# RWKV7 attention into a mixture of experts: raw V and R of the fourth unit loaded ahead of its raw W, those of the fifth behind it, and both turned ahead of the decay for tokens

## The chip, the cores and the metric

The kernel runs on one core of a Trainium2 chip. The metric is the device time of one execution in microseconds (us); less is better. The core has a matrix engine (TensorE, PE in the profile), three engines for elementwise work (VectorE or DVE, ScalarE or ACT, GpSimd or POOL), and SyncE (SP), which here issues nearly all DMA transfers. Each engine works through its own list of instructions in order; engines wait for one another by semaphores.

## The reference

Two stages follow one another. The first is a recurrence over time for each batch and head, with a 40 x 40 state:

```python
# r, k, v, w, a, b: (B=4, H=8, S=768, D=40) float32
for t in range(S):
    y[:, :, t] = einsum('bhd,bhde->bhe', rt, state)
    Sa = einsum('bhde,bhe->bhd', state, at)
    state = state * wt[:, :, None, :] - einsum('bhd,bhe->bhde', Sa, bt)
    state = state + einsum('bhd,bhe->bhde', vt, kt)
```

The second takes y as x with N = 3072 tokens and D = 320 features through a mixture of E = 4 experts with F = 1024 hidden features:

```python
p = domain_probs / (domain_probs.sum(-1, keepdims=True) + 1e-09)
for e in range(E):
    h = maximum(x @ w1[e], 0.0)
    out += p[:, e:e + 1] * (h @ w2[e])
```

## The kernel before

**Units.** Time is cut into 12 chunks of 64 steps and the batch into 2 pairs, so there are 24 units; unit u is chunk u // 2 of pair u % 2, with 16 sequences (2 batches of 8 heads). Inside a unit the recurrence is replaced by matrices: products of W up to each step (G), scores between the steps of the unit, and a triangular system that is solved by doubling in Z and M. Between units of one pair only the state is passed on. When a unit's Y is there, its tokens go through the experts, in pieces that are put between the attention's steps to keep TensorE fed.

**Stages of a unit.** The generator `within` (from line 407) prepares a unit in stages, each ended by a `yield`:

- Stage 1 turns raw W (as loaded, features not yet on the partitions) into G with VectorE's 32 x 32 stream transpose (`turn_raw`, L245) and scans it to running products (L443).
- Stage 2 is the decay for tokens: TensorE turns G back to tokens (`pg`), VectorE multiplies by natural W (`gp`, L454) and takes the reciprocal (L455).
- Stage 3 makes `n_tok` (L476) and `k_tok` (L481) from gp and natural B and K, turns raw A into `AT` (L245) and multiplies it by G (L485), copies natural V into `VC`, and, from unit 3 on, turns raw V and R into `VT` and `RT` by `turn_rv`.
- Stage 4 has TensorE turn n_tok and k_tok (`pNT`, `pKT`), ScalarE copy them out (`NT`, `KT`), TensorE multiply RT with VT (`pc`, the scores of R against V) and NT and KT with AT (`pfe`), and VectorE copy the causal halves (`VC`, `ET`).

`PADDED` is 3: units 0 to 2 bring V and R in by another way (padded tiles turned by TensorE), and unit 3, the fourth, is the first to load them raw. `EARLY` is 5.

After that `substitute` solves the triangular system (M on VectorE, Z on GpSimd, L585 and L598), `merge` turns the result (`Qc`, `QTc`, then `pY`, `Yq`, `pQ`), and `step` carries the state on (`prn`, `RH`, `psat`, `SX`, `pxr`, `pdy`, Y, state). In `mixture_of_unit` and `mixture_of_chunk` TensorE makes `ph`, ScalarE applies the ReLU (`hs`), TensorE makes `po` or `p`, and VectorE evicts it with the gate into `osb` (L795, L797). From later units on VectorE also adds pairs of hs into `a` (L903), and the experts' weights are summed accordingly (`sums`, `w`, L869).

**Buffers.** Raw W, A, R and V have one buffer each: a unit's raw tile can be loaded when the unit before has turned its own. VT, NT and KT share three buffers, RT has two, AT two. PSUM for the experts has three buffers (two for ph, one for p or po).

**Order.** TensorE's instructions run in the order of the program. On VectorE, ScalarE and SP a scheduler sets the order from its own estimate of times, save where `pin` keeps an instruction behind the one before it: in `within` up to unit 3 (L411) and, for G, again from unit 8. From unit 4 on the stages' instructions on VectorE are therefore the scheduler's to place.

**Loads.** `load_raw` returns the issues of a unit's raw tiles in the order of the letters it is given: 4 issues for W or A, 8 for V or R, since the sequences of V and R are put in another order for the two halves. The runs of one issue are 72 or 48 floats long. `go` issues them on SP at once; what is in `later` is issued by `begin_later`, in the next turn of the loop. In the code, unit 3's raw W is issued while unit 2 is prepared, raw A, V and R after its natural tiles; in the loop over u, unit u + 3 has raw W and A issued at once and raw V and R put into `later`.

Of the kernel before, what the change touches and what calls it, by code (L numbers as in the profile page):

```python
# [15 lines left out]
def kernel(  # L16
# [145 lines left out]
    PADDED = 3  # L162
# [27 lines left out]
    units = []  # L190

    def begin(u):
        q = Unit()
        q.u, q.c, q.bp = u, u // (B // 2), u % (B // 2)
        q.b = [2 * q.bp, 2 * q.bp + 1]
        q.start, q.end = q.c == 0, q.c == NC - 1
        q.apart = u >= EARLY + 2
        q.n = {}
        units.append(q)
        return q  # L200
# [38 lines left out]
    def go(moves, eng=None):  # L239
        for move in moves:  # L240
            move(eng or nc.sync)
# [106 lines left out]
    def by(x, n):  # L348
        return x.rearrange("p (h e) -> p h e", e=n)
# [3 lines left out]
    def turn(name, src, pinned=False):  # L353

        p = big(name)
        for j in range(NJ):
            ins = transpose(out=p[:, j * P:(j + 1) * P], in_=src(j), identity=ident[:])
            if pinned and j == 0:
                tc.keep_in_program_order(ins)
        return p  # L360

    def tok(x):
        return lambda j: x[:, 2 * j:2 * j + 2, :].rearrange("p h e -> p (h e)")
# [42 lines left out]
    def within(q):  # L406
# [10 lines left out]
        ahead = G[:, 1:2 * NJ * L + 1].rearrange("p (j i t) -> p i j t", i=2, t=L)  # L417
# [21 lines left out]
        if q.u == 1:  # L439
            yield  # L440
            VT = turn_rv()
# [7 lines left out]
            pin(turn_raw(q.AT[:], n["rawA"][:]))  # L449
        yield  # L450

        pg = by(turn("pg", tok(Gv), q.u == 2)[:], 64)[:, :, 0:D]
        gp = sb.tile([P, H, D], FP32, name="gp")
        pin(nc.vector.tensor_tensor(out=gp[:], in0=pg, in1=n["W"][:], op=ALU.mult))  # L454
# [32 lines left out]
        q.VC = VCs()  # L487
        if q.u > 0:
            nc.scalar.copy(out=q.VC[:, :, 0:D], in_=token_V())
        if q.u >= PADDED:  # L490
            VT = turn_rv()
        yield

# [2 lines left out]
        if q.u == 2:  # L496
            VT = turn_rv()
# [49 lines left out]
    def substitute(q, eng, between=None, during=None):  # L547

        blocks = sb.tile([P, H, Q], FP32, name="blocks")
        for i in range(P // Q):  # L550
            move = nc.scalar.copy if i >= 2 else nc.vector.tensor_copy
            tc.keep_in_program_order(move(out=blocks[quarter(i)], in_=q.F[quarter(i), :, quarter(i % 2)]))  # L552
        q.below = belows()
        for i in (1, 3):
            tc.keep_in_program_order(nc.gpsimd.tensor_copy(out=q.below[quarter(i)], in_=q.F[quarter(i), :, 0:Q]))  # L555
        M = sb.tile([P, Q, Q], FP32, name="M")
        cols = blocks[:].rearrange("p h c -> p c h")[:, :, None, :].to_broadcast([P, Q, 4, H])
        ins = nc.vector.transpose(out=M[:], in_=cols)  # L558
        tc.keep_in_program_order(ins)


        pairs = M[:].rearrange("p (c two) r -> p c two r", two=2)
        on_diag = M[:].rearrange("p c r -> p (c r)")[:, Q + 1::2 * (Q + 1)]
        tc.keep_in_program_order(nc.vector.memset(on_diag, 0.0))

        Z = sb.tile([P, 4, Q // 4, Q], FP32, name="Z")
        q.Z = Z[:, 0]
        by_second = Z[:, 1:3].rearrange("p x k r -> p (x k) r")
        below = M[:].rearrange("p c r -> p (c r)")[:, 1::2 * (Q + 1)]
        ins = nc.vector.tensor_tensor(  # L570
            out=by_second, in0=pairs[:, :, 1, :], in1=below[:, :, None].to_broadcast([P, Q // 2, Q]), op=ALU.mult,
        )
        tc.keep_in_program_order(ins)
        ins = nc.vector.tensor_tensor(out=pairs[:, :, 0, :], in0=pairs[:, :, 0, :], in1=by_second, op=ALU.add)  # L574
        tc.keep_in_program_order(ins)
        run(between)
        at_once = eng is nc.vector
        for x in (0, 3) if at_once else (0,):
            tc.keep_in_program_order(eng.tensor_copy(out=Z[:, x], in_=unit_cols[:]))
        for j in range(0, Q, 2):  # L580
            if during:
                during(j)
            n, m = j // 4 + 1, Q - 1 - j
            here = 3 * (j // 2 % 2) if at_once else 0
            ins = eng.tensor_tensor(  # L585
                out=Z[:, 1:3, 0:n, j + 1:Q], in0=M[:, j:j + 2, None, j + 1:Q].to_broadcast([P, 2, n, m]),
                in1=Z[:, here, 0:n, j:j + 2].rearrange("p k x -> p x k")[:, :, :, None].to_broadcast([P, 2, n, m]),
                op=ALU.mult,
            )
            if j == 0:  # L590
                tc.keep_in_program_order(ins)
            z = Z[:, :, 0:n, j + 1:Q]
            if at_once:
                terms = z[:, 0:3] if here == 0 else z[:, 1:4]
                eng.tensor_reduce(out=z[:, 3 - here], in_=terms.rearrange("p x k r -> p k r x"), op=ALU.add, axis=AX.X)  # L595
            else:
                for x in range(1, 3):
                    eng.tensor_tensor(out=z[:, 0], in0=z[:, 0], in1=z[:, x], op=ALU.add)  # L598
        if at_once:

            odd, even = (Z[:, x].rearrange("p k (r four) -> p k r four", four=4)[:, :, :, 1:3] for x in (3, 0))
            eng.tensor_copy(out=even, in_=odd)
# [431 lines left out]
    def scores_of(u):  # L1034
        run(ws[u], 1)
        yield
# [34 lines left out]
    def during_second(j):  # L1071
# [4 lines left out]
        if j == 12:  # L1076
            run(norm)

    substitute(units[1], nc.vector, scores_of(1), during_second)
    m, s = merge(units[1]), begin_step(1)  # L1080
    run(m, 1)
    run(ws[2], 1)
    go(load_raw(begin(3), "W"))
    mix(2)
    run(ws[2], 1)
    run(m, 1)
# [4 lines left out]
    run(s, 2)  # L1091
    run(ws[2], 1)
    load(units[3], "WBKV")
    go(load_raw(units[3], "AVR"))
    run(ws[2], 2)
    substitute(units[2], nc.gpsimd)
    mix(1)
# [8 lines left out]
    for u in range(1, NU):  # L1106
        in_order[0] = True
        q = units[u]
        m = s_next = w = w_next = iter(())
        if u + 1 < NU:  # L1110
            m, s_next = merge(units[u + 1]), begin_step(u + 1)
            w_next = ws[u + 1]
        if u + 2 < NU:
            w = ws[u + 2]

        def gap(n, pieces=None):
            at = 4 * u + n
            run(sum_ops, sums_at.get(at, 0))
            mix((1 if at in sparse else 2) if pieces is None else pieces)

        early = u < EARLY
        if early:
            begin_later(len(later))
        ahead = u + 3 < NU and u in range(EARLY, EARLY + 3)
        if ahead:
            go(load_raw(begin(u + 3), "W"))
        if early:
            lead()
        run(w_next, 99 if early else 1)
        run(s, 1)  # L1130
        gap(0)


        if early:
            run(s, 1)
        run(w, 1)
        if not early:
            run(w_next)
            run(s)

        if early:
            run(w, 1)
            gap(1, 2 if u + 1 == EARLY else None)
            run(s)
        if u == 1:
            mixture_of_unit(q)
        elif q.bp:
            mixture_of_chunk(units[u - 1:u + 1], chunks_x[q.c])
        if not early:
            begin_later(len(later))  # L1150
            run(w, 1)
            lead()
            todo[:2] = todo[1::-1]
            gap(1)
            run(m, 1)

        if u + 3 < NU:
            go(load_raw(units[u + 3] if ahead else begin(u + 3), "A" if ahead else "WA"))
            load(units[u + 3], "WBKV")
            later.extend(load_raw(units[u + 3], "VR"))  # L1160
        run(w, 2)

        soon = u in (2, 3, 4)
        if soon:
            run(w, 1)
        if early:
            run(m, 1)
        else:
            run(m, 1)
            run(s_next, 1)  # L1170
            lead()
            run(m, 1)
            if u + 3 < NU:
                ws.append(within(units[u + 3]))
                run(ws[u + 3], 1)
        if soon:
            substitute(units[u + 2], nc.gpsimd)
        gap(2)

        if u == 1:  # L1180
            run(s_next, 1)
            run(m, 1)
        if not soon:
            run(w, 1)
        if not soon and u + 2 < NU:
            with sooner(not early):
                substitute(units[u + 2], nc.gpsimd)
        if not early:
            lead()
            run(s_next, 1)  # L1190
        if early:
            run(w, 1)
        if early:
            ws.append(within(units[u + 3]))
            run(ws[u + 3], 1)
            if u > 1:
                run(m, 1)
                run(s_next, 1)
            run(m)
            gap(3, 1)  # L1200
            run(s_next, 1)
        else:
            begin_later(len(later))
            gap(3)
        s = s_next
# [31 lines left out]
```

## Time and profile before

| | |
|---|---|
| median of 3 runs | 1095.37 us (1095.02 to 1099.68) |
| the profiled execution | 1096.91 us |
| its span in the profile | 1095.2 us |
| mean granted TensorE clock | 0.988 |
| TensorE's idle time where it waits for turned R (100 to 330 us) | 2.2 us in 2 waits |
| SP's issues of unit 3's raw V and R | 91.71 to 101.35 us |
| SP's issues of unit 4's raw V and R | 123.34 to 132.90 us |

The profile is one execution; its times are microseconds from the start of its span, and 1.7 us lie around the span. A line of the timeline gives start, duration, engine, line of the kernel, operation, output <- inputs, and in brackets the idle time of the engine before it with what ended it. "issue" there is a wait for nothing that the profile shows.

### The profile page before, as it was taken

Reading aid. Unit: us, or ns where it says so; the run is one execution under the profiler, and the core shown is the slowest. Engines: PE = TensorE matmul, PEld = TensorE weight load, DVE = VectorE, ACT = ScalarE, POOL = GpSimd, SP = SyncE. Lnnn points to the kernel's source line nnn. Section 1 sums busy time; section 2 is a strip of 40 time slices with the busy share of each in tenths; the row PEclk is TensorE's granted clock in tenths of the full one; section 3 lists DMA queues with packets and bytes.
Section 4 is the critical chain, followed back from the end, with each engine's and each line's share of the span. In section 5 each row is a group of like instructions: output and inputs, shape, how many; then the busy total and the mean of one; then the engine's idle time right before and its main releaser. Section 6 shows DMA issues by size and latency. Waiting matters only on the chain.

```text
span 1095.2 us, 38536 instructions
## 1 busy us (share of the span) xinstructions
PE 1068.1 (98%) x16102; PEld 959.0 (88%) x16102; DVE 759.0 (69%) x1551; ACT 353.4 (32%) x956; POOL 490.3 (45%) x1274
## 2 busy tenths in 40 slices
PE   7798999999999999999999999999999999999998
PEld 6677788889998999999999999989999999998887
DVE  7676569887776777767768768767777676544343
ACT  2432444234223333333233242343333332221110
POOL 5206577763472562653643634735625536420000
PEclk8799999999999999999999999999999999999999
DMA  7876545434444463454454454444543532322320
GB/s 118 236 231 142 131 91 131 107 77 108 120 119 105 110 144 97 103 146 97 100 133 105 106 122 106 115 99 105 131 103 85 149 89 60 99 71 79 107 75 13
DMA packets 268869, 122.19 MB, mean 112 GB/s; under 512 B 213736, under 2 KB 242072, under 8 KB 268696
## 3 DMA queue, kind: packets, MB, share of 16 engines
q1 hardware_dynamic: 265416, 119.12, 43.4%
q8 instruction: 127, 2.08, 0.8%
q10 hardware_dynamic: 3280, 0.61, 0.4%
q14 instruction: 46, 0.38, 0.1%
HBM read 111.79 MB, written 3.93 MB: 106 GB/s over the span
## 4 chain that ended last, share of the span: by engine, by line
PE 92%; DVE 4%; ACT 1%; DMA 1%; issue 1%; SPq 0%; DVEq 0%; ACTq 0%
PE ph L76 39%; PE p L76 31%; PE pdy L76 3%; PE psat L76 2%; PE pxr L76 2%; PE po L76 2%; PE prn L76 2%; PE pfe L76 1%; PE pc L76 1%; PE pQ L76 1%; PE pev L76 1%; PE pg L79 1%; PE pY L76 1%; DVE Z L595 1%; PE pe L76 1%
## 5 line engine op out<-in xcount | busy, mean ns | idle before, releaser
L76 PE MATMUL ph<-xT,w1p 128*128 128x256 f32 (+3 forms) x3040 | 443.9, 375 | 3.7 <-issue 3.6
L76 PEld LDWEIGHTS ph<-xT,w1p 64*64 64x64 f32 (+1 forms) x3040 | 337.7, 162 | 59.3 <-issue 18.9
L598 POOL TENSOR_TENSOR Z<-Z 128x31 f32<-128x31 f32 (+7 forms) x704 | 254.8, 362 | 55.2
L903 DVE TENSOR_TENSOR a<-hs 128x512 f32<-128x512 f32 x220 | 153.3, 714 | 105.9 <-ACT hs L784 105.9
L784 ACT ACTIVATE hs<-ph 128x512 f32<-128x512 f32 (+1 forms) x208 | 117.1, 564 | 332.0 <-PE ph L76 331.7
L585 POOL TENSOR_TENSOR Z<-M,Z 128x62 f32<-128x62 f32 (+7 forms) x352 | 148.6, 422 | 99.0 <-DVE M L574 73.1
L76 PE MATMUL p<-sums,a 128*128 128x160 f32 x1056 | 164.9, 299 | 0.0
L76 PEld LDWEIGHTS p<-sums,a 128*128 128x128 f32 x1056 | 152.8, 190 | 2.2
L797 DVE SCALAR_TENSOR_TENSOR osb<-p,gate,osb 128x320 f32<-128x320 f32 (+1 forms) x243 | 108.0, 481 | 62.6 <-PE p L76 57.5
L555 POOL COPY below<-F 32x256 f32<-32x256 f32 x48 | 21.4, 446 | 232.2 <-ACT F L511 230.6
L76 PEld LDWEIGHTS p<-w,hs 128*128 128x128 f32 x704 | 98.6, 190 | 8.5 <-issue 7.3
L76 PE MATMUL p<-w,hs 128*128 128x160 f32 x704 | 104.9, 302 | 0.0
L76 PE MATMUL p<-w,a 128*128 128x160 f32 x704 | 102.8, 299 | 0.0
L76 PEld LDWEIGHTS p<-w,a 128*128 128x128 f32 x704 | 98.0, 190 | 0.0
L617 POOL COPY QT<-QTc 32x256 f32<-32x256 f32 x96 | 40.4, 421 | 81.9 <-DVE QTc L611 68.7
L706 ACT COPY RS<-pxr 64x256 f32<-64x256 f32 x88 | 32.2, 366 | 99.7 <-DVE SX L404 66.6
L540 ACT COPY EV<-pev 64x160 f32<-64x160 f32 x96 | 23.0, 286 | 91.6 <-PE pev L76 91.2
L455 DVE RECIPROCAL gp<-gp 128x320 f32<-128x320 f32 x24 | 51.6, 2151 | 0.7
L404 DVE COPY_PREDICATED VC<-mask_up,pc 128x256 f32<-128x256 int32 x48 | 18.7, 442 | 45.4 <-PE pc L76 45.3
L558 DVE STREAM_TRANSPOSE M<-blocks 128x1024 f32<-128x1024 f32 x24 | 47.2, 1969 | 2.9 <-ACT blocks L552 2.4
L511 ACT COPY F<-pfe 128x256 f32<-128x256 f32 x48 | 15.5, 376 | 80.9 <-PE pfe L76 79.3
L76 PE MATMUL pdy<-VC,k_tok 64*64 64x104 f32 (+1 forms) x768 | 38.2, 259 | 0.0
(149 smaller groups left out, 1343.9 us busy)
## 6 DMA issues: line engine op xcount, KB each, us to landing
w1p<-in_moe_w_dram SPq DMA_DIRECT2D x95, 512.0 KB
w1p<-in_moe_w_dram SPq DMA_DIRECT2D x190, 64.0 KB
w<-in_moe_w_dram SPq DMA_DIRECT2D x4, 1280.0 KB
sums<-in_moe_w_dram SPq DMA_DIRECT2D x9, 512.0 KB
natW<-in_w_dram SPq DMA_DIRECT2D x48, 80.0 KB
natB<-in_b_dram SPq DMA_DIRECT2D x48, 80.0 KB
natK<-in_k_dram SPq DMA_DIRECT2D x48, 80.0 KB
out_dram<-osb SPq DMA_DIRECT2D x46, 80.0 KB
```

Source lines behind the costliest of these rows:

```text
L76: return stated(nc.tensor.matmul(**k))
L455: pin(nc.vector.reciprocal(out=gp[:], in_=gp[:]))
L540: nc.scalar.copy(out=of_slot(q.EV[half(p)], i ^ p)[:, :, 0:D], in_=pev[i][half(p)])
L555: tc.keep_in_program_order(nc.gpsimd.tensor_copy(out=q.below[quarter(i)], in_=q.F[quarter(i), :, 0:Q]))
L558: ins = nc.vector.transpose(out=M[:], in_=cols)
L585: ins = eng.tensor_tensor(out=Z[:, 1:3, 0:n, j + 1:Q], in0=M[:, j:j + 2, None, j + 1:Q].to_broadcast([P, 2, n, m]), in1=Z[:, here, 0:n, j: ...
L598: eng.tensor_tensor(out=z[:, 0], in0=z[:, 0], in1=z[:, x], op=ALU.add)
L617: ins = nc.gpsimd.tensor_copy(out=q.QT[quarter(i), :, quarter(i % 2)], in_=QTc[quarter(i)])
L706: nc.scalar.copy(out=RS[half(s), x ^ s::2], in_=prs[x][half(s)].rearrange("p (j i) t -> p j i t", i=2),)
L784: nc.scalar.activation(out=h[:, i * HF // 2:(i + 1) * HF // 2, 0:n], in_=ph[i][:], func=ACTF.Relu,)
L797: nc.vector.scalar_tensor_tensor(out=to, in0=p, scalar=sc, in1=to, op0=ALU.mult, op1=ALU.add)
L903: nc.vector.tensor_tensor(out=t[:], in0=x, in1=y, op=op)
```

## The change

Raw V and R of unit 3 are issued in the code ahead of unit 1's substitution, and so ahead of unit 3's raw W, which stays where it was; raw A stays too. Unit 4's raw tiles are all issued at once, in the order W, V, R, A, in place of W and A at once and V and R in `later`. In `within`, `turn_rv` of these two units is called ahead of stage 2's `pg`, `gp` and reciprocal in place of the end of stage 3. Units from 5 on keep their calls. No instruction is added or taken away, and no buffer changes its size.

```diff
@@ within(q)
+        rv_first = q.u in (PADDED, PADDED + 1)
+        if rv_first:
+            VT = turn_rv()
         pg = by(turn("pg", tok(Gv), q.u == 2)[:], 64)[:, :, 0:D]
         gp = sb.tile([P, H, D], FP32, name="gp")
         pin(nc.vector.tensor_tensor(out=gp[:], in0=pg, in1=n["W"][:], op=ALU.mult))
...
         if q.u > 0:
             nc.scalar.copy(out=q.VC[:, :, 0:D], in_=token_V())
-        if q.u >= PADDED:
+        if q.u >= PADDED and not rv_first:
             VT = turn_rv()
         yield
@@ ahead of the loop over units
+    begin(3)
+    go(load_raw(units[3], "VR"))
     substitute(units[1], nc.vector, scores_of(1), during_second)
     m, s = merge(units[1]), begin_step(1)
     run(m, 1)
     run(ws[2], 1)
-    go(load_raw(begin(3), "W"))
+    go(load_raw(units[3], "W"))
...
     load(units[3], "WBKV")
-    go(load_raw(units[3], "AVR"))
+    go(load_raw(units[3], "A"))
@@ in the loop over units
         if u + 3 < NU:
-            go(load_raw(units[u + 3] if ahead else begin(u + 3), "A" if ahead else "WA"))
+            rv_now = u + 3 == PADDED + 1
+            go(load_raw(units[u + 3] if ahead else begin(u + 3), "A" if ahead else "WVRA" if rv_now else "WA"))
             load(units[u + 3], "WBKV")
-            later.extend(load_raw(units[u + 3], "VR"))
+            if not rv_now:
+                later.extend(load_raw(units[u + 3], "VR"))
```

In the orders that result, TensorE's and GpSimd's instructions are as before. SP issues unit 3's 16 transfers of V and R between two pieces of w1p, at about 50 us of the profile's time, and unit 4's 16 directly behind its raw W. On VectorE, unit 3's VT stands behind unit 2's AT, its RT behind the copies to SX, and its AT with the multiply behind QTc. Unit 4's VT and RT stand ahead of Y, and behind the updates of the state come the eviction `osb` of po, AT with its multiply, `sums`, and then gp, the reciprocal, n_tok and k_tok; before, gp, the reciprocal, VT, n_tok and k_tok stood ahead of that `osb`. In unit 5 RT falls behind an `osb`; in unit 9 AT's turn comes ahead of two additions `a`, in unit 10 ahead of RH; further shifts are of neighbours.

## The prediction

> **What bounds the kernel now.** I read the page's first part and its chain of waits, then the waits of TensorE, then the timelines of TensorE and VectorE around units 3 and 4. Busy time and chain first:
>
> ```profile
> PE 1068.1 (98%) x16102; PEld 959.0 (88%) x16102; DVE 759.0 (69%) x1551; ACT 353.4 (32%) x956; POOL 490.3 (45%) x1274
> ...
> PE 92%; DVE 4%; ACT 1%; DMA 1%; issue 1%; SPq 0%; DVEq 0%; ACTq 0%
> ```
>
> TensorE (PE) sets the end; VectorE (DVE) is on the chain for 4%. So the change is worth what it does to PE's idle gaps. The waits of PE from 100 to 330 us (instruction, what it waited for, us in total, times, longest):
>
> ```profile
> PE ph L76 <- issue: 2.9, 2, 1.6
> PE pc L76 <- DVE RT L245: 2.2, 2, 1.8
> ```
>
> The second line is what the change touches: twice PE waits for the turned R, 2.2 us in all. From 400 us to the end the same view shows no wait of PE, so no gap there can take a delay back: what PE loses early is lost. PE's timeline has the two places (start, duration, then in brackets idle time before it and its releaser), unit 3 first:
>
> ```profile
> 105.49 0.69 PE L76 MATMUL pc<-RT,VT 40*64 40x64 f32 x32 [1.80 <-DVE RT L245]
> ...
> 132.91 4.47 PE L76 MATMUL po<-w,hs 128*128 128x320 f32 x16
> 137.22 1.50 PE L76 MATMUL pxT<-Y,sums 128*128 128x128 f32 x12
> 138.63 0.66 PE L79 MATMUL pNT<-ident,n_tok 128*128 128x128 f32 x4
> ...
> 140.21 0.69 PE L76 MATMUL pc<-RT,VT 40*64 40x64 f32 x32 [0.36 <-DVE RT L245]
> ```
>
> PE runs pNT at 138.63 without a wait: n_tok was just ready. VectorE's timeline shows why:
>
> ```profile
> 113.98 0.56 DVE L660 TENSOR_TENSOR RH<-prn,EV 128x160 f32<-128x160 f32 x2 [2.13 <-PE prn L76]
> ...
> 135.37 2.14 DVE L455 RECIPROCAL gp<-gp 128x320 f32<-128x320 f32 x1
> ...
> 138.01 0.56 DVE L476 SCALAR_TENSOR_TENSOR n_tok<-natB,gp 128x320 f32<-128x320 f32 x1
> ...
> 139.00 0.54 DVE L797 SCALAR_TENSOR_TENSOR osb<-po,gate,osb 128x320 f32<-128x320 f32 x1
> ```
>
> In unit 4 the reciprocal runs beside po's 4.47 us of matmuls; the eviction osb, which needs po's end at 137.38, comes after n_tok.
>
> [...] The trace agrees that VectorE does not pass such an instruction: RH holds it 2.13 us though G's turns, whose raw W was issued by 106.9, stand next in line. [...] the trace: 2.14 us for 128x320 against 0.47 us for gp's multiply of the same size. [...] raw V and R move 288 B and 192 B runs (72 and 48 floats). The page counts 213736 of 268869 packets under 512 B, but no PE wait here names such a load, so I put no price on it.
>
> **The change part by part.** The order of instructions on each engine follows from the two programs. PE and GpSimd keep theirs. ScalarE moves only the copy of natV for units 3 and 4, three copies back; natV's column is first read by pdy many us later, so nothing.
>
> 1. Loads of unit 3. The 16 issues of raw V and R (9.6 us of SP's queue, 91.71 to 101.35) move to about 50 us, into a stretch where SP is idle from 57.2 to 68.55. The weight issues behind them (a w1p piece, sums, w: 54.30 to 57.2) slip by up to 9.6 us into that idle stretch; I estimate their first users at 75 us, 8 us after they are issued. Cost nothing, at worst 1 us if one of them is late. The nine issues of sums that stood behind at 101.44 come some 9 us earlier: nothing waits for them.
>
> 2. Turns of unit 3. VT moves to about 82 us, where DVE sits idle 8.36 us until pc; RT into the 2.87 us before Y (96.56). So the wait of 1.80 us goes. But AT's turn and multiply (0.70 + 0.69) now stand behind QTc: Qc waits for GpSimd's Z (3.70 us in VectorE's timeline, until 110.75), which PE's gain does not move; QTc ends at 111.86, AT is ready at 113.25. PE, 1.80 us earlier, reaches pfe (before: 114.04) at about 112.3 and waits there to 113.3; RH, also behind AT, runs at 113.25 instead of 113.98. pQ then follows at about 114.9 against 115.73. Net -0.8 us. Bounds: -1.8 if Z comes earlier too, -0.2 if RH is the tighter one.
>
> 3. Loads of unit 4. Its 16 issues (9.5 us, 123.34 to 132.90) move ahead of raw A and the natural W, B, K, V (107 to 117.7). These then issue 9.5 us later, up to about 118 to 127, after some 5 to 9 us gained from part 1; they are needed from 120.67 (AT) and 134.74 (gp). Nothing, up to +0.5. PE's unexplained 1.58 us before ph at 127.12 lies in the stretch the loads leave; it may go with them (-1.6) or turn up elsewhere. I take 0.
>
> 4. Order of VectorE in unit 4, the largest term. In the new order osb (po) stands ahead of AT's turn and multiply, sums, gp, reciprocal, n_tok. The osb waits for po's end, 137.38. From there, by distance from start to start: osb 0.46, AT 0.65 and 0.6, sums 0.7, gp 0.5, reciprocal 2.1, n_tok 0.56: 5.6 us, so n_tok is ready at 143.0 and PE, ready for pNT at 138.63, waits 4.4 us. The 0.36 us of RT goes, since RT is turned long before: pNT, pKT, pc follow at 143.0, 143.6, 144.2 against 140.21. Net +4.0 us (3.3 without sums in between, 4.6 with semaphore delays). While PE waits, GpSimd and ScalarE run on, so small waits that follow may go (pxr for SX, 0.6 us in two places in the view of waits): -0.4, between 0 and -0.65.
>
> 5. Unit 5 keeps its loads but its RT falls behind osb: pc waits about +0.4 (0 to 0.7).
>
> 6. Later order. In unit 9 (around 298 us) AT's turn moves ahead of two multiplies a. These lines show the place:
>
> ```profile
> 298.37 0.71 DVE L245 STREAM_TRANSPOSE AT<-rawA 128x512 f32<-128x512 f32 x1 [0.93 <-DMA rawA<-in_a_dram]
> ...
> 300.04 0.38 DVE L797 SCALAR_TENSOR_TENSOR osb<-p,minus_gate,osb 128x160 f32<-128x160 f32 x1
> ...
> 300.28 1.11 PE L76 MATMUL ph<-xT,w1p 64*64 64x256 f32 x13
> ```
>
> ph at 300.28 takes the PSUM that this osb frees at 300.42. The two a (1.29 us) and AT's multiply (0.6) now fall between 299.07 and it: +1.9 us, or nothing if raw A lands 2 us earlier relative to PE. Its issue at 294.78 stands behind xT's transfers of Y, so it moves with PE; I take +1.9. In unit 10 AT's turn (before at 340.16, after 3.85 us of waiting for raw A) moves ahead of RH; one more of raw A's issues goes before xT's, so it lands about 2 us earlier, and what hangs on it is late by +0.5 (0.25 to 0.9).
>
> Sum: -0.8 + 4.0 - 0.4 + 0.4 + 1.9 + 0.5 = +5.6 us. The profiled execution took 1096.91 us (span 1095.2 and 1.7 around it), 1.5 above the median of 1095.37. The terms are differences, so I put them on the median: 1101.0.
>
> **The rivals.**
> A, not slower: the decay of unit 4 is not late, because DVE reaches gp before po ends. Place: pNT at 138.63. It decides from the point where n_tok is ready by 138.6, which needs gp to start by about 135.5. For it: gp's operands are ready at 132.9 in the trace. Against: the order puts osb ahead and DVE does not pass it. Then 4.4 us fall out of the sum: 1096.6, or, with parts 5 and 6 also absorbed and the whole 1.80 kept, 1095.4 - 2.2 = 1093.2.
> B, partly given back: the decay is late as worked out, but units 9 and 10 take no harm, because raw A lands earlier than PE comes: 5.6 - 2.4 = +3.2, so 1098.6. For it: SP's queue is lighter in places. Against: the waits for raw A of 0.93 and 3.85 us in the trace.
> C, heavier: unit 3 gains only 0.2, unit 4 loses 4.6, unit 10 0.9: +0.6 +0.6 +0.4 on the sum, and 0.5 from part 3: +7.7, so 1103.1.
>
> **How the numbers follow.** Forecast 0.58, C 0.16, B 0.14, A 0.12. A change of 0.5%, about what a measurement of this kernel can tell from none, is 5.5 us: the lines are 1089.9 and 1100.85. The forecast lies just above the upper one; of its 0.58, with 1099.0 to 1103.0 as its own range, I put 0.34 above and 0.24 within. Slower: 0.34 + 0.16 = 0.50. Within: 0.24 + 0.14 + 0.09 = 0.47. Faster, a corner of A with the 1.58 us gone as well: 0.03. The range takes in B, C and A's upper value: 1096.6 to 1103.8.
>
> **What would show it.** In the new trace: no wait of pc for RT in units 3 and 4 (part 2); pfe waiting for AT about 1 us near 113; pNT near 138 waiting 4 to 4.6 us for n_tok on VectorE, with osb ahead of the reciprocal (part 4); an extra wait of ph near 305, PSUM freed by osb (part 6). No gap at pNT would make the forecast wrong by most of its size; a raw A that lands before VectorE gets to it would undo part 6.

## The result and the profile after

The changed kernel took 1105.05 us in the median of six runs (1103.13 to 1106.53), the kernel before 1097.05 us in six runs (1094.26 to 1099.68), three of which are those of the table above. The ratio is 1.0072, with a 95% interval of 1.005 to 1.0095: about 8 us slower. The profiled execution took 1106.13 us, its span 1104.4 us against 1095.2 before. The forecast was +5.6 us, or 1101.0 with a range of 1096.6 to 1103.8; the direction held, the size was too small.

The page of the changed kernel, busy time and chain of waits:

```profile
PE 1069.2 (97%) x16102; PEld 958.4 (87%) x16102; DVE 760.4 (69%) x1551; ACT 353.7 (32%) x956; POOL 493.2 (45%) x1274
...
PE 86%; DVE 4%; DMA 3%; issue 2%; SPq 2%; ACT 2%; POOL 2%; ACTq 0%; DVEq 0%; POOLq 0%
```

Each engine is busy for as long as before within 3 us; TensorE's share of the chain fell from 92% to 86%. The time is in waits. Those of TensorE from 140 to 420 us (what waited for what: us in total, times, longest):

```profile
PE pNT L79 <- DVE n_tok L479: 4.7, 1, 4.7
PE ph L76 <- issue: 3.6, 3, 1.9
PE p L76 <- ACT hs L787: 1.1, 1, 1.1
```

The first line did not exist before. On TensorE's timeline the places are (start, duration, in brackets the idle time before and what ended it):

```profile
111.56 0.68 PE L76 MATMUL pY<-QTc,below 64*64 64x64 f32 x16 [1.12 <-DVE QTc L614]
112.98 0.69 PE L76 MATMUL pfe<-NT,AT 64*64 64x64 f32 x32 [0.74 <-DVE AT L488]
...
141.41 1.12 PE L79 MATMUL pNT<-ident,n_tok 128*128 128x128 f32 x4 [4.66 <-DVE n_tok L479]
...
307.30 0.87 PE L76 MATMUL ph<-xT,w1p 64*64 64x256 f32 x11 [1.94 <-issue]
...
349.85 1.35 PE L76 MATMUL p<-w,a 128*128 128x160 f32 x8 [1.12 <-ACT hs L787]
```

The 1.80 us of pc for RT are gone; QTc and AT, 1.86 us together, took their place. The large wait is that of pNT in unit 4. VectorE's timeline shows what n_tok stood behind:

```profile
132.87 0.32 DVE L735 TENSOR_TENSOR state<-state,gl 128x160 f32<-128x160 f32 x1
135.45 0.55 DVE L800 SCALAR_TENSOR_TENSOR osb<-po,gate,osb 128x320 f32<-128x320 f32 x1 [2.26 <-PE po L76]
135.92 0.70 DVE L245 STREAM_TRANSPOSE AT<-rawA 128x512 f32<-128x512 f32 x1
136.66 0.69 DVE L488 TENSOR_TENSOR AT<-AT,G 128x512 f32<-128x512 f32 x1
137.27 0.92 DVE L872 TENSOR_TENSOR sums<-w 128x640 f32<-128x640 f32 x1
138.11 0.48 DVE L457 TENSOR_TENSOR gp<-pg,natW 128x320 f32<-128x320 f32 x1
138.62 2.15 DVE L458 RECIPROCAL gp<-gp 128x320 f32<-128x320 f32 x1
140.81 0.55 DVE L479 SCALAR_TENSOR_TENSOR n_tok<-natB,gp 128x320 f32<-128x320 f32 x1
```

VectorE stands idle for 2.26 us at osb, which needs po; gp stands three more operations behind it. Most of gp and the reciprocal (0.48 and 2.15 us) would have fitted into that idle time; before, they ran while po ran.

The wait at 307.30 lies inside a group of ph, behind its first two matmuls. The view names no releaser ("issue"), but VectorE's order gives one:

```profile
303.35 0.71 DVE L245 STREAM_TRANSPOSE AT<-rawA 128x512 f32<-128x512 f32 x1 [4.67 <-DMA rawA<-in_a_dram]
303.99 1.25 DVE L906 TENSOR_TENSOR a<-hs 128x512 f32<-128x512 f32 x2
...
306.82 0.38 DVE L800 SCALAR_TENSOR_TENSOR osb<-p,minus_gate,osb 128x160 f32<-128x160 f32 x1
```

AT stands ahead of the two additions a and waits 4.67 us for raw A, and this osb, whose PSUM ph takes, ends at 307.20, 0.10 us ahead of the matmul. In late_order and vr_behind_natural below the distance from the end of this osb to the matmul is 0.10 us too.

The same instructions of TensorE, set side by side by their place in its order, give the difference of their starts, after less before. It is -0.15 us at 83 us, -1.10 at pfe of unit 3, -1.98 at 126 us, +2.78 at pNT of unit 4, +3.77 at 145 us, +4.29 at 192 us, +4.49 at 300, +6.79 at 307, +8.39 at 313 and +9.67 at 350; at the end +9.26. After pNT's wait and after that at 307 the difference goes on growing, though TensorE does not wait. The granted clock, the share of TensorE's full clock that the profile records as granted, shows why (columns: stretch of time, its length, TensorE's busy time and instructions, granted clock, DMA share, GB/s):

```profile
138.00:141.40 3.40, 0.00 (x0) 1.00 0.53 95
141.40:144.80 3.40, 3.39 (x64) 0.50 0.47 77
144.80:148.20 3.40, 3.40 (x92) 1.00 0.68 114
305.20:308.60 3.40, 1.46 (x45) 1.00 0.71 113
308.60:312.00 3.40, 3.40 (x56) 0.51 0.83 225
```

After each of the two waits TensorE runs one stretch of 3.4 us at half its clock. By the starts the first cost 1.0 us (1.3 us, less 0.3 us for the wait for RT that is gone), the second 1.6 us. The kernel before has one such stretch too, also worth 1.6 us, behind its own wait of 1.80 us at 105.49:

```profile
103.50:106.90 3.40, 1.60 (x53) 1.00 0.92 270
106.90:110.30 3.40, 3.40 (x24) 0.51 0.88 176
```

### The profile page after: what moved, and what is told of

It is laid out like the page before. It is cut to its first block, busy times and chain, and to the rows that moved or that the text cites. A ratio compares the mean times of both kernels' runs of the same rounds, so it can differ in the third digit from the quotient of the medians.

```text
span 1104.4 us, 38533 instructions
## 1 busy us (share of the span) xinstructions
PE 1069.2 (97%) x16102; PEld 958.4 (87%) x16102; DVE 760.4 (69%) x1551; ACT 353.7 (32%) x956; POOL 493.2 (45%) x1274
## 4 chain that ended last, share of the span: by engine, by line
PE 86%; DVE 4%; DMA 3%; issue 2%; SPq 2%; ACT 2%; POOL 2%; ACTq 0%; DVEq 0%; POOLq 0%
PE ph L76 37%; PE p L76 30%; PE pdy L76 3%; PE psat L76 2%; PE pxr L76 2%; PE pfe L76 1%; PE prn L76 1%; PE po L76 1%; PE pc L76 1%; PE pQ L76 1%; POOL Z L601 1%; PE pY L76 1%; PE pe L76 1%; PE pev L76 1%; PE pg L79 1%
## 5 line engine op out<-in xcount | busy, mean ns | idle before, releaser
L601 POOL TENSOR_TENSOR Z<-Z 128x31 f32<-128x31 f32 (+7 forms) x704 | 259.3, 368 | 55.2
L588 POOL TENSOR_TENSOR Z<-M,Z 128x62 f32<-128x62 f32 (+7 forms) x352 | 145.5, 413 | 97.3 <-DVE M L577 71.4
```

The costliest lines, as they stand in the source:

```text
L588: ins = eng.tensor_tensor(out=Z[:, 1:3, 0:n, j + 1:Q], in0=M[:, j:j + 2, None, j + 1:Q].to_broadcast([P, 2, n, m]), in1=Z[:, here, 0:n, j: ...
```

## The experiments

Theory 1 was that the loss lies in VectorE's order: unit 4's decay behind osb, and AT ahead of its neighbours in units 9 and 10. The rivals were the transfers themselves, the earlier calls of the turns, and chance in the clock. Diffs are against the changed kernel unless said otherwise; the ratio is always to the kernel before, run beside it on the same chip.

**u3_alone**: unit 3's part without unit 4's.

```diff
-        rv_first = q.u in (PADDED, PADDED + 1)
+        rv_first = q.u == PADDED
...
-            rv_now = u + 3 == PADDED + 1
+            rv_now = False
```

> Only unit 3's part of the change: its raw V and R early, its turns early; unit 4 as before. Theory 1 (the loss is VectorE's order in unit 4 and in units 9 and 10, which this kernel does not have): no wait of pc for RT in unit 3, about 1.1 us of QTc and 0.7 us of AT in its place near 111 to 113 us, no wait of pNT near 138, none near 307 or 350; 1 to 3 us faster than before. Rival (the early transfers of raw V and R disturb the weights or the natural tiles): no gain, 1 us or more slower.

Ratio 0.9997 (0.9984 to 1.001). The waits are where theory 1 put them (QTc 1.09, AT 0.74, none at pNT), and there was a half-clock stretch behind those two, at 111.8 us. But no gain is left where 1 to 3 us were expected: unit 3's part gives back at QTc and AT what it takes from RT. The rival's slowdown isn't there either.

**loads_only**: the loads of the change with the old calls of the turns.

```diff
-        rv_first = q.u in (PADDED, PADDED + 1)
+        rv_first = False
```

> The loads of both units as in the changed kernel, the calls that turn V and R where they were before. Theory 1 (the order of the loads in SP's queue alone makes the scheduler put osb ahead of gp): pNT of unit 4 waits 4 to 5 us as in the changed kernel, time within 1.5 us of it. Rival (the earlier call of the turns displaces gp): wait under 1 us, time within 3 us of before.

Ratio 1.0076 (1.0055 to 1.0097), pNT waits 3.77 us, a little under the 4 to 5 expected: the loss is that of the changed kernel within these intervals. VectorE's order is nearly the same too, osb and AT ahead of gp, only `sums` ahead of osb; the wait is shorter by 0.89 us, about what `sums` takes. Half clock follows it here for two stretches (139.91 to 146.74), which cost 2.1 us in the starts. So where `turn_rv` is called counts for little, and the order of the loads for nearly all.

**nat_first**: unit 4's natural tiles ahead of all its raw ones.

```diff
+            if rv_now:
+                begin(u + 3)
+                load(units[u + 3], "WBKV")
+                go(load_raw(units[u + 3], "WVRA"))
+            else:
...
```

> The whole change, but unit 4's natural W, B, K, V are issued ahead of its raw W, V, R, A. VectorE's order then has gp and the reciprocal of unit 4 ahead of osb again; the order in units 9 and 10 stays that of the changed kernel. Theory 1: the 4.7 us wait of pNT near 141 us is gone (under 0.5), the waits near 307 (1.9) and 350 (1.1) stay, the time lies 2 to 4.5 us above before. Rival (the transfers of V and R themselves make the natural tiles late): pNT still waits over 2 us, or gp waits for a DMA; 6 to 9 us above before.

Ratio 1.0073 (1.0054 to 1.0093). The wait of pNT went, to 0.25 us, as theory 1 had it. Its time was wrong: with raw A now last in SP's queue, AT stands behind QTc, and the wait moved on to pfe. VectorE and, below it, TensorE of this run:

```profile
136.71 0.47 DVE L457 TENSOR_TENSOR gp<-pg,natW 128x320 f32<-128x320 f32 x1
...
143.39 0.45 DVE L614 STREAM_TRANSPOSE QTc<-Qc 128x256 f32<-128x256 f32 x1
143.76 0.67 DVE L245 STREAM_TRANSPOSE AT<-rawA 128x512 f32<-128x512 f32 x1
144.46 0.88 DVE L488 TENSOR_TENSOR AT<-AT,G 128x512 f32<-128x512 f32 x1
```

```profile
140.20 0.66 PE L79 MATMUL pNT<-ident,n_tok 128*128 128x128 f32 x4 [0.25 <-DVE n_tok L479]
...
145.49 0.69 PE L76 MATMUL pfe<-NT,AT 64*64 64x64 f32 x32 [3.48 <-DVE AT L488]
```

AT shows no wait for a transfer when its turn comes, and neither did gp in the changed kernel. The tile that SP issues last is the one whose use ends up late in VectorE's order, though the data are there. That the scheduler does this because it expects the transfer later than it comes is the likely reading; its estimate was not seen.

**vr_behind_natural**: one edit, raw V and R of unit 4 behind its natural tiles.

```diff
-            go(load_raw(units[u + 3] if ahead else begin(u + 3), "A" if ahead else "WVRA" if rv_now else "WA"))
+            go(load_raw(units[u + 3] if ahead else begin(u + 3), "A" if ahead else "WA"))
             load(units[u + 3], "WBKV")
+            if rv_now:
+                go(load_raw(units[u + 3], "VR"))
```

> The whole change with one edit: unit 4's raw V and R are issued behind its natural tiles in place of directly behind its raw W. Theory (in the changed kernel gp of unit 4 was late because the scheduler took natural W to be late behind these 16 issues): no wait over 0.6 us at pNT and pfe near 140 us, 4.5 to 6 us less than the changed kernel, so 1.5 to 4 us above before; the wait near 305 us stays about 2 us. Rival (the loss comes from elsewhere): within 2 us of the changed kernel.

Ratio 1.0002 (0.9987 to 1.0017), about 7.7 us less than the changed kernel by the two ratios, more than the 4.5 to 6 expected; the wait in unit 10 (p for hs) is gone too. gp runs beside po again and osb comes after:

```profile
131.92 0.47 DVE L457 TENSOR_TENSOR gp<-pg,natW 128x320 f32<-128x320 f32 x1
132.31 0.31 DVE L735 TENSOR_TENSOR state<-state,gl 128x160 f32<-128x160 f32 x1
132.54 2.14 DVE L458 RECIPROCAL gp<-gp 128x320 f32<-128x320 f32 x1
134.61 0.51 DVE L800 SCALAR_TENSOR_TENSOR osb<-po,gate,osb 128x320 f32<-128x320 f32 x1
135.03 0.48 DVE L479 SCALAR_TENSOR_TENSOR n_tok<-natB,gp 128x320 f32<-128x320 f32 x1
```

TensorE shows no wait at pNT or pfe of unit 4; only pc waits 0.50 us for RT. The wait in unit 9 is there, 2.20 us with its half-clock stretch.

**gp_behind_osb**: a case in between: osb stays ahead of gp, but nothing else stands between them.

```diff
-            if q.u <= PADDED or also:
+            if q.u <= PADDED + 1 or also:
```

> The changed kernel with unit 4's instructions on VectorE kept in the program's order as those of units up to 3 are: osb still ahead of gp, but AT, its multiply and sums behind k_tok. n_tok then follows po's end by osb 0.5, gp 0.5, reciprocal 2.15 and n_tok 0.5, in all 3.7 us in place of 5.9: the wait of pNT falls from 4.7 to about 2.5 us, still followed by half clock, and the time lies 1.5 to 3 us below the changed kernel unless pfe then waits for AT behind k_tok or QTc (AT needs 1.3 us more, pfe comes 1.7 us after pNT). Rival (the wait depends on a transfer and not on what stands between): pNT waits 4 us or more.

pNT waits 2.42 us; ratio 1.0037 (1.0017 to 1.0058). The wait is as worked out from what stands between po's end and n_tok, so it depends on that and not on a transfer. The time lies about 3.8 us under the changed kernel's by the ratios, a little more than expected; the two intervals just overlap.

**late_order**: vr_behind_natural, and unit 3's raw A behind its natural W and B, so that neither unit's AT falls behind QTc; units 9 and 10 in the order of the changed kernel.

> The whole change, but with unit 4's raw V and R issued behind its natural tiles, and unit 3's raw A behind its natural W and B. VectorE's order then has no AT behind QTc in units 3 and 4 and gp of unit 4 ahead of osb; the order in units 9 and 10 is that of the changed kernel. Theory (the later order alone costs what the trace showed there): no wait over 0.6 us at pNT and pfe near 138 to 146 us, TensorE 1 to 3 us ahead of before at 200 us, then +2.5 us near 307, up to +1.4 of half clock behind it, +1.5 near 350: 2 to 4.5 us slower than before. Rival (the later waits were a consequence of unit 4's delay): no waits over 0.8 us near 300 and 345, time within 1 us of before or faster.

Ratio 0.9993 (0.9978 to 1.0008). The wait in unit 9 came as expected, 1.92 us, with VectorE's order its cause and no delay of unit 4 needed for it. But the whole was not slower: no half-clock stretch followed, and unit 10 showed no wait at p. In the changed kernel unit 10 lost 1.3 us because AT waited for raw A until 346.63, RH stood behind AT, and ScalarE's copy SN, with hs behind it, waited 5.82 us for RH. Here AT got raw A at 335.54 and nothing was late. In gp_behind_osb, where AT came at 344.86, there is no wait at p either. So this loss needs more than the order. The time that SP took for the 12 transfers of Y ahead of the last part of raw A goes with it: 10.66 us in the changed kernel, where p waited 1.12 us; 10.01 us in nat_first, where p waited 0.75 us; 8.9 to 9.1 us in loads_only, vr_behind_natural, gp_behind_osb and late_order, all with AT directly ahead of RH, where p did not wait. Why SP takes longer in some executions is open, and with it how often that loss comes.

**gaps**: waits of chosen length put into the kernel before, where TensorE otherwise waits for nothing.

```diff
         pin(nc.vector.reciprocal(out=gp[:], in_=gp[:]))
+        for _ in range({12: 9, 14: 11, 16: 13, 18: 15, 20: 17, 22: 20}.get(q.u, 0)):
+            nc.vector.tensor_scalar(out=gp[:], in0=gp[:], scalar1=1.0, scalar2=None, op0=ALU.mult)
```

> The kernel before, with 9, 11, 13, 15, 17 and 20 multiplications of gp by 1.0 put behind the reciprocal of units 12, 14, 16, 18, 20 and 22, where n_tok has about 3.75 us to spare; each takes about 0.46 us, so TensorE's waits there grow from about 0.5 to 5 us. Clock theory: each wait of about 1.8 us or more is followed by one stretch of 3.4 us in which the granted clock is 0.5, and none under 1.6 us is; the time grows by 1 to 1.5 us for each such wait beyond the waits themselves. Rival (such stretches fall without regard to waits): as many as before, one, wherever it falls, and the time grows by the sum of the waits alone.

This kernel was executed once. Units 12 and 14 gave waits of 0.69 and 1.21 us, of pY for QTc; of the next four units, TensorE's lines:

```profile
634.74 0.63 PE L79 MATMUL pNT<-ident,n_tok 128*128 128x128 f32 x4 [1.33 <-DVE n_tok L478]
...
722.89 0.63 PE L79 MATMUL pNT<-ident,n_tok 128*128 128x128 f32 x4 [2.39 <-DVE n_tok L478]
...
813.24 1.09 PE L79 MATMUL pNT<-ident,n_tok 128*128 128x128 f32 x4 [3.60 <-DVE n_tok L478]
...
905.03 0.75 PE L79 MATMUL pNT<-ident,n_tok 128*128 128x128 f32 x4 [4.92 <-DVE n_tok L478]
```

and the stretches around them (columns as above):

```profile
631.30:634.70 3.40, 2.11 (x10) 1.00 0.10 26
634.70:638.10 3.40, 3.04 (x118) 1.00 0.10 21
721.10:724.50 3.40, 1.61 (x44) 1.00 0.07 18
724.50:727.90 3.40, 3.40 (x100) 0.50 0.23 44
809.80:813.20 3.40, 0.00 (x0) 1.00 0.10 23
813.20:816.60 3.40, 3.36 (x52) 0.51 0.27 53
902.00:905.40 3.40, 0.36 (x4) 1.00 0.08 19
905.40:908.80 3.40, 3.40 (x77) 0.50 0.67 192
```

The three waits over 2.3 us are each followed by one stretch at half clock, that of 1.33 us is not; each stretch cost 1.6 us more in the starts of the instructions. The span grew by 22.7 us: the six waits, with 0.31 us of pY in unit 16, make 14.5, the three stretches 4.8, and one more stretch near 212 us 1.7; the other 1.7 us are the balance of smaller gains and losses. Chance in the clock does not give that. One part of the expectation failed: the stretch near 212 us follows a wait called issue of 1.51 us, less than the 1.6 us under which none was expected. The bounds of 1.8 and 1.6 us fit the kernel before, where half clock follows the wait of 1.80 us and not that of 1.58. The cost of a stretch lies a little above the 1 to 1.5 us expected.

**u3_a_sooner and v_now_r_later**: what is left when the losses are kept out. The first is u3_alone with raw A of unit 3 sooner; the second adds raw V, not R, of unit 4 at once, behind its natural tiles, and keeps the early turns of both units. The edit of the second:

```diff
-    load(units[3], "WBKV")
+    load(units[3], "WB")
     go(load_raw(units[3], "A"))
+    load(units[3], "KV")
...
-            go(load_raw(units[u + 3] if ahead else begin(u + 3), "A" if ahead else "WVRA" if rv_now else "WA"))
+            go(load_raw(units[u + 3] if ahead else begin(u + 3), "A" if ahead else "WA"))
             load(units[u + 3], "WBKV")
-            if not rv_now:
-                later.extend(load_raw(units[u + 3], "VR"))
+            if rv_now:
+                go(load_raw(units[u + 3], "V"))
+            later.extend(load_raw(units[u + 3], "R" if rv_now else "VR"))
```

> Unit 3's part alone, and its raw A issued behind natural W and B instead of behind K and V. VectorE's order then has unit 3's AT and its multiply ahead of Qc and QTc again. Theory (the gain of unit 3 was given back by AT standing behind QTc, and by the stretch at half clock that follows these waits): no wait of pfe for AT near 112, the wait of pY for QTc may stay at up to 1.1 us, no half-clock stretch between 100 and 125 us, 1.5 to 3 us faster than before. Rival (the gain is lost to something else, such as the wait of ph near 127 us that the profile calls issue): within 1 us of before, with a wait of 2 us or more at 127.

> Unit 3 as in u3_a_sooner; of unit 4 only raw V is issued at once, behind its natural tiles, and raw R stays in later. VectorE's order in units 9 and 10 is then that of before, gp of unit 4 stands ahead of osb, VT ahead of gp and only RT behind k_tok. Theory: no wait of pc for RT, none over 0.6 us at pNT, the wait near 300 us under 1 us, no half-clock stretch between 60 and 400 us: 2 to 4 us faster than before. Rival (what is gained is lost at the waits called issue and by the later order anyway): within 1 us of before.

Ratios 0.9979 (0.997 to 0.9989) and 0.9976 (0.9965 to 0.9986): 2.3 and 2.6 us faster than before, both clear of no change, and not to be told from each other. In u3_a_sooner AT runs at 103.35, ahead of QTc; pfe does not wait, pY waits 1.62 us for QTc where at most 1.1 was expected, and there is no half-clock stretch in the middle of the kernel at all. In v_now_r_later pc has no wait for RT in units 3 and 4, but the expectation that no half-clock stretch falls between 60 and 400 us failed: one follows a wait of 1.83 us called issue at 124.47. These waits come and go from kernel to kernel (1.58 us at 127.12 before, none in the changed kernel, 2.25 us at 126.33 in u3_alone), always at the same matmul of ph. The traces give a hint: in before, u3_alone and v_now_r_later it starts 1.4 us after a 16 KiB packet of the DMA queue q8, "instruction" on the page, has landed (at 125.70 in before, 124.97 in u3_alone, 123.11 in v_now_r_later); in the changed kernel that packet landed at 122.62, ahead of the start of this group of ph at 123.14. Whether TensorE waits for that packet was not shown; no run tested it.

## Why the prediction was right in direction and too small

- Part 1, the early loads of unit 3 at no cost: held. At 83 us the starts differ by 0.15 us. One reading was off without consequence: six issues of sums stood at 101.44, not nine; the other three came at 117.77.
- Part 2, -0.8 us at unit 3: the starts of pQ moved from 115.73 to 114.59, -1.1 us. The reason was half right. AT behind QTc was there. Not in the sum were the wait of pY for QTc (1.12 us) and the half-clock stretch of the kernel before, 1.6 us, which went together with the wait of 1.80 us. That the two nearly cancel is luck.
- Part 3, no price on the unexplained wait before ph: it went in the changed kernel, and 0.59 us for hs came in its place, some -0.9 us net.
- Part 4, the largest term: the mechanism was right line by line, and the wait was 4.66 us against 4.4 worked out. What failed is the size of the term "+4.0", which priced a wait of TensorE at its own length. From ahead of pNT to behind pfe the starts moved by 5.7 us, for the wait was followed by 1.3 us of half clock. The small waits that were to give back 0.4 us stayed (pxr for SX, 0.6 us in two places, as before). The 0.6 us for semaphore delays in the upper figure, 4.6, was the author's estimate; here pNT starts 0.05 us after n_tok ends.
- Part 5, unit 5: pc waits 0.31 us more, against 0.4.
- Part 6, "+1.9" and "+0.5": the mechanism in unit 9 was right (the two a are additions, and ph waits behind its first two matmuls), and so was the wait, 1.94 us, or 2.3 us in the starts. The term failed as that of part 4 did: 1.6 us of half clock followed, which the sum did not have. Unit 10 gave 1.3 us in this one execution, through RH and ScalarE's queue behind AT; four other kernels with AT ahead of RH did not lose it.

So the step that failed is the price of a wait of TensorE: parts 4 and 6 took its length alone, and the half clock behind the two waits added 2.9 us. The starts in the profiled executions sum to: -1.1 us at unit 3, -0.9 by 128 us, +5.7 in unit 4, +0.7 up to 300 us, +2.3 and +1.6 in unit 9, +1.3 in unit 10, -0.4 after it: +9.2 us, 3.6 more than forecast. Units 4 and 9 make 3.7 of that difference. These are two single executions; by the ratio of the runs, on the 1095.37 us that the prediction stood on, the change is +7.9 us, or 1103.3. The median of before in the six runs, 1097.05, lies 1.7 us above that base, which lifts the measured time by as much.

Of the rivals, A fell: VectorE did not pass osb, and stood at it for 2.26 us though gp's pg had ended at 131.11. B, the later units unharmed, fell in this profile. C named an outcome near the measured size, with other reasons for it: it had unit 3 gain only 0.2 us, where it gained 1.1, and it had no half clock. Theory 1 is shown by vr_behind_natural and gp_behind_osb for unit 4, its largest part; for unit 9 the wait itself is shown twice; for unit 10 the order alone does not give the loss.

## What to carry to other kernels

Where a scheduler places an engine's instructions, moving a load can move instructions that do not use it: in these runs the tile issued last was used late, and where its user stands in order behind an eviction that waits for the matrix engine, that wait becomes the user's. So put new early loads behind the tiles that are needed first (here that took the loss away and gave no gain of its own: vr_behind_natural is as fast as before), and read the engine's new order for every instruction that comes to stand behind a waiting one. And price a wait of TensorE above its length: most of those here that left it idle for about half of a stretch of 3.4 us, or more, were followed by half clock, and one stretch of it cost 1.3 to 1.7 us more.

## What the runs showed of the hardware

Waits of TensorE of 1.80 us (before, 105.49), 1.94 (changed kernel, 307.30) and 2.20 (vr_behind_natural, 299.63) were followed by a stretch at half clock. The length of the wait does not decide, for u3_alone's of 2.25 us, at 126.33, had none behind it. In all eleven traces the changes of the granted clock lie on one grid of 3.41 us per trace (before: 42.08, 106.94 and 110.35 us; changed kernel: 42.41, 141.39, 144.81, 308.65 and 312.06), and what tells most cases apart is how much of a stretch of that grid TensorE was busy. Between 60 and 1080 us there are 18 stretches at full clock whose next one is at half clock; in 16 of them TensorE was busy for 0.00 to 1.73 us, in the other two for 1.89 (gaps, 209.1) and 1.90 (gp_behind_osb, 141.7). The bound is not sharp: stretches with 1.78 us (changed kernel, 110.7), 1.83 (before, 124.0) and once even 1.51 (gaps, 898.6) were followed by full clock. u3_alone's wait fell on two stretches (1.98 and 2.57 us busy), and late_order's of 1.92 us left its stretch at 2.07:

```profile
294.70:298.10 3.40, 2.81 (x48) 1.00 0.61 105
298.10:301.50 3.40, 2.07 (x79) 1.00 0.75 143
```

So nearly the same wait cost 1.9 us there and, with 1.6 us of half clock, 3.5 us in the changed kernel, by where it fell. Whether part of the spread between runs of one kernel comes from this was not measured.
